# Convolution of the later blocks in 64-token pieces on eight array tiles

## The chip, the cores and the metric

The kernel runs on one core of a Trainium2 chip. The metric is the device time in microseconds (us) of one execution, taken as the median of several runs. A core has a matrix engine (TensorE, PE in the profile, its weight loads PEld), a vector engine (VectorE, DVE), an activation engine (ScalarE, ACT), a general engine (GpSimd, POOL) and a queue that issues transfers (SyncE, SP). Each works through its own list of instructions; semaphores tie the lists together.

## The reference

Two operations follow each other. First a dynamic convolution: each token and head has 7 weights, normalised by a softmax, which are applied to the token and its 6 predecessors, separately for each of 8 heads of 24 channels. Then a feed-forward network with squared relu.

```python
# x: (8, 4096, 192), weight_gen: (8, 4096, 8, 7)
w = softmax(weight_gen, axis=-1)
x_pad = concatenate([zeros((B, 6, D)), x], axis=1)
x_unf = x_pad[:, idx, :].reshape(B, S, K, H, group)     # idx: token + 0..6
y = einsum('bshk,bskhg->bshg', w, x_unf)                # (8, 4096, 192)
h = maximum(y.reshape(32768, 192) @ w_in, 0.0)          # w_in: 192 x 2048
out = (h * h) @ w_out                                   # w_out: 2048 x 192
```

## The kernel before

The 32,768 tokens are cut into 64 sub-blocks of 512 tokens. The first two blocks hold one sub-block each, all others two; there are 33 blocks. A hand-written plan (a string for each block, with "u" for a unit of the first product, "M" for half a quarter of the second, "C" for the convolution of the next block, "B" for bands, "E" and "S" for pieces of the softmax, "L" for a load) sets the order in which every engine's instructions are issued. Blocks from the fifth on use one fixed pattern, and from the one ahead of the ninth block on it is this one:

```python
steady_spread = "MuMuuu" * 2 + "MuCMuuu" + "MuMuuu"
```

So a block is 16 units and eight halves, and the next block's convolution stands between a unit and an L621 half, about the middle of it. The second product that "M" issues belongs to a block issued earlier.

*Softmax and rows.* The softmax weights of a batch are computed with tokens on partitions and stored to memory (`vd`) with 8 slots a head; `wr_load` brings them back for a sub-block as NT = 5 overlapping tiles of 128 tokens, 104 apart (STEP), through SyncE. `x_load` brings the same rows of x as fp16 through GpSimd. Both use `block_load`, which needs one transfer, or two where the first or last tile starts elsewhere. Both are issued two blocks ahead of their block: rows at a block's start, x behind a convolution, since x has two buffers.

*Bands.* `st_band` (L395, VectorE) multiplies the rows with a banded mask, so that the 7 weights of a token become a column of a 128 x 104 band matrix, for each head and tile. `st_bands` does this in one operation for tiles of like offset, up to 4,160 elements a partition.

*Convolution.* `st_conv_spread` (from block 8, FIRST_SPREAD, on; blocks count from 0) multiplies x by the bands on TensorE: 128 token rows contracted, 32 channels out, 104 or 96 tokens wide. Four such matmuls, for two sub-blocks and two heads, go to the four column tiles of the array. The results go to two accumulators `yp` from a ring of three (`ps_h`, shared with the first product), and ScalarE and VectorE copy one each to `y` (L503). A head has 24 channels and a tile 32 places; the spare 8 places of six heads hold a third each of the last two heads. These are computed as a fourth slot and moved to the spare places by transfers on SyncE (L507), and the weights of the first product, `w_p`, are loaded in the same arrangement (`load_w_spread`).

*First product.* `st_unit` issues six matmuls of 64 rows x 512 columns (L572): three slots, each on the upper and the lower half of the array. ScalarE applies the relu (L586), VectorE squares (L590).

*Second product.* `st_mm2` (L621) contracts 128 hidden values in two halves of 64 rows, side by side, 192 columns each; 32 matmuls for an "M". `o_sum` adds the halves, `o_store` writes the result.

*Head.* TensorE starts with 21 matmuls of 512 columns on zeros (`spin`), while the first weights are loaded and the first softmax is computed. GpSimd builds the row selection and the mask, issues loads, and clears `v_big`.

The softmax here doesn't subtract the row's maximum and nothing guards it: scores larger than these inputs give would overflow.

## Time and profile before

| What | us |
|---|---|
| Median of 3 runs | 732.07 |
| Lowest, highest | 731.87, 732.11 |
| Profiled execution, whole | 731.82 |
| Profiled execution, span | 730.0 |

The span runs from the first to the last instruction. Groups of instructions are named by line, engine, operation and tile, with the count behind an x; then come the sum of their times in us, the mean of one in ns, and the idle time of the engine just ahead of them with its releaser. The costliest groups besides those that the next section shows:

```profile
L586 ACT ACTIVATE t<-h 128x1024 f16<-128x1024 f32 x512 | 496.4, 1026 | 60.3 <-PE h L572 58.8
L621 PE MATMUL o<-w_o,g 64*128 64x192 f16 x7872 | 365.5, 243 | 0.1
L590 DVE TENSOR_TENSOR g<-t 128x2048 f16<-128x2048 f16 x225 | 267.4, 1220 | 29.8 <-ACT t L586 29.7
L572 PE MATMUL h<-y,w_p 64*128 64x512 f16 x2400 | 291.7, 376 | 0.0
L395 DVE TENSOR_TENSOR bd<-wr,mask 128x4160 f16<-128x4160 f16 x41 | 94.9, 2316 | 0.1
L395 DVE TENSOR_TENSOR bd<-wr,mask 128x3328 f16<-128x3328 f16 x21 | 39.6, 1884 | 0.1
L493 PE MATMUL yp<-bd,xt 128*32 128x104 f16 x1600 | 27.3, 211 | 0.0
L493 PE MATMUL yp<-bd,xt 128*32 128x96 f16 x400 | 22.7, 206 | 0.0
```

"64*128" is the part of the array that an instruction uses, rows by columns. Busy time is a union: matmuls that overlap count once. The mean of one is its latency, so it says nothing of how close together they can start.

### The profile page before, as it was taken

What the parts mean: (1) busy time and instruction counts of PE and PEld (TensorE: products, weight loads), DVE (VectorE), ACT (ScalarE), POOL (GpSimd) and SP (SyncE); (2) the same over time, 40 slices, a digit from 0 to 9 for tenths busy, and PEclk for the clock granted to TensorE, in tenths of its full rate; (3) what the DMA queues carried; (4) which work ended last, traced back from release to release, by engine and by line L of the source; (5) the groups of instructions that cost most, each with busy time, mean ns of one, the idle gap of its engine ahead of it and who ended that gap; (6) DMA issues with size and microseconds to landing.
All of it is one profiled execution on the core that took longest, in us unless ns stands there. A gap on an engine that the chain in (4) does not pass through costs nothing.

```text
span 730.0 us, 30988 instructions
## 1 busy us (share of the span) xinstructions
PE 724.1 (99%) x14053; PEld 528.0 (72%) x14053; DVE 626.8 (86%) x836; ACT 612.2 (84%) x733; POOL 99.8 (14%) x145
## 2 busy tenths in 40 slices
PE   8999999999999999999999999999999999999998
PEld 4657788777777777777777777777777777777777
DVE  7998998998898988888988888988889988778753
ACT  5999888888888888888888888888888888888883
POOL 8131223321001100011001010010000110001000
PEclk9999999999999999999999999999999999999999
DMA  9555455685345452455432554343544325444012
GB/s 202 118 105 115 82 96 105 132 149 129 86 66 138 90 92 59 82 117 124 76 64 61 136 104 88 56 77 116 107 84 86 57 52 119 66 87 78 30 45 68
DMA packets 125984, 68.30 MB, mean 94 GB/s; under 512 B 85321, under 2 KB 122140, under 8 KB 125340
## 3 DMA queue, kind: packets, MB, share of 16 engines
q0 software_dynamic: 46192, 19.43, 22.9%
q1 hardware_dynamic: 79516, 46.79, 22.4%
q8 instruction: 110, 1.80, 1.1%
q14 instruction: 22, 0.18, 0.1%
q10 hardware_dynamic: 144, 0.10, 0.0%
HBM read 50.18 MB, written 28.70 MB: 108 GB/s over the span
## 4 chain that ended last, share of the span: by engine, by line
PE 98%; ACT 1%; DVE 0%; DMA 0%; issue 0%
PE o L621 47%; PE h L572 44%; PE yp L493 4%; PE h L557 2%; PE yp L527 1%; DMA wg<-in_weight_gen_dram 0%; PE yp L455 0%; ACT y L538 0%; DVE v_first L260 0%; PE pr L372 0%; ACT t L586 0%; DVE ssum L245 0%; ACT ex L238 0%; DVE rcp L252 0%; ACT wr L381 0%
## 5 line engine op out<-in xcount | busy, mean ns | idle before, releaser
L586 ACT ACTIVATE t<-h 128x1024 f16<-128x1024 f32 x512 | 496.4, 1026 | 60.3 <-PE h L572 58.8
L621 PEld LDWEIGHTS <-g 64*128 64x128 f16 (+1 forms) x8032 | 344.3, 94 | 55.0 <-issue 2.2
L621 PE MATMUL o<-w_o,g 64*128 64x192 f16 (+1 forms) x8032 | 380.1, 243 | 0.1
L590 DVE TENSOR_TENSOR g<-t 128x2048 f16<-128x2048 f16 (+1 forms) x287 | 307.4, 1105 | 30.1 <-ACT t L586 29.9
L572 PE MATMUL h<-y,w_p 64*128 64x512 f16 x2400 | 291.7, 376 | 0.0
L572 PEld LDWEIGHTS <-w_p 64*128 64x128 f16 x2400 | 113.9, 94 | 94.7
L395 DVE TENSOR_TENSOR bd<-wr,mask 128x4160 f16<-128x4160 f16 (+4 forms) x90 | 149.6, 1686 | 1.3 <-ACT wr L381 0.7
L637 DVE TENSOR_TENSOR o_sb<-o,o_sb 128x384 f32<-128x384 f32 x123 | 68.4, 556 | 61.1 <-ACT o_sb L635 60.1
L321 POOL DMA_DIRECT2D xt<-in_x_dram x63 | 52.6, 839 | 415.3 <-PE yp L493 362.5
L635 ACT COPY o_sb<-o 128x384 f32<-128x384 f32 x129 | 61.6, 477 | 45.9 <-PE o L621 45.1
L572 PE MATMUL h<-y,w_i 64*128 64x512 f16 x576 | 70.6, 376 | 0.3 <-ACT t L586 0.3
L572 PEld LDWEIGHTS <-w_i 64*128 64x128 f16 x576 | 30.3, 94 | 22.2 <-issue 1.6
L493 PEld LDWEIGHTS <-xt 128*32 128x32 f16 x2000 | 24.6, 95 | 10.6 <-issue 10.6
L260 DVE TENSOR_TENSOR v_big<-ex,rcp 128x112 f16<-128x112 f32 (+5 forms) x180 | 29.9, 237 | 1.7 <-DMA vd<-v_big 0.7
L503 DVE CAST y<-yp 128x1024 f16<-128x1024 f32 x25 | 30.4, 1218 | 0.0
L493 PE MATMUL yp<-bd,xt 128*32 128x104 f16 (+1 forms) x2000 | 28.4, 210 | 0.0
L238 ACT ACTIVATE ex<-wg 128x560 f32<-128x560 f32 (+4 forms) x38 | 25.9, 682 | 1.9 <-DMA wg<-in_weight_gen_dram 1.9
L245 DVE TENSOR_REDUCE ssum<-ex 128x80 f32<-128x560 f32 (+4 forms) x38 | 25.3, 666 | 1.3 <-ACT ex L238 1.3
L503 ACT CAST y<-yp 128x1024 f16<-128x1024 f32 x25 | 25.2, 1007 | 0.0
L252 DVE RECIPROCAL rcp<-ssum 128x80 f32<-128x80 f32 (+4 forms) x38 | 22.8, 600 | 1.3
L311 POOL DMA_DIRECT2D xt<-in_x_dram x7 | 3.9, 554 | 120.9 <-PE yp L493 109.4
L355 POOL DMA_DIRECT2D wr<-v_first x24 | 12.9, 560 | 25.1 <-DVE v_first L260 13.6
(41 smaller groups left out, 115.1 us busy)
## 6 DMA issues: line engine op xcount, KB each, us to landing
out_dram<-o_sb SPq DMA_DIRECT2D x63, 384.0 KB
xt<-in_x_dram POOLq DMA_DIRECT2D x42, 240.0 KB, 4.7
wg<-in_weight_gen_dram SPq DMA_DIRECT2D x4, 1064.0 KB
xt<-in_x_dram POOLq DMA_DIRECT2D x21, 192.0 KB, 5.2
wr<-vd SPq DMA_DIRECT2D x38, 80.0 KB
vd<-v_big SPq DMA_DIRECT2D x5, 512.0 KB
y<-y SPq DMA_DIRECT2D x100, 24.0 KB
wg<-in_weight_gen_dram SPq DMA_DIRECT2D x3, 616.0 KB
```

Source lines behind the costliest of these rows:

```text
L238: nc.scalar.activation(out=self.ex[:, lo:hi].rearrange("p r g k e -> p (r g) k e"), in_=self.wg[:, lo:hi].rearrange("p r (g e) k -> p (r g ...
L260: eng.tensor_tensor(out=bass.AP(tensor=v.tensor, offset=v.offset + lo * H * SL + lo % SL * 2 + g * SL * 2, ap=[list(v.ap[0]), [H * SL + 2, ...
L321: eng.dma_start(out=dst[:, first:last], in_=ap)
L395: nc.vector.tensor_tensor(out=bd_t[j][:, H * lo : H * (lo + len(tiles) * n)].rearrange("p (g m c) -> p g m c", g=shape[1], c=2 * SL), in0= ...
L493: nc.tensor.matmul(out=yp[p0 : p0 + 32, k - k0, a:b], lhsT=x_t[s][:, i, c0 : c0 + 32], rhs=bd[:, head // 2, e, 0 : b - a], start=True, sto ...
L503: copy(out=y[:, k0 : k0 + 2], in_=yp)
L572: nc.tensor.matmul(out=h[:, half], lhsT=w_in_chunk(w, u, slot, half), rhs=y_t[j][r0 : r0 + RT, k], start=(slot == 0), stop=(slot == NK - 1 ...
L586: nc.scalar.activation(out=t1[:, e], in_=h, func=ActF.Relu)
L590: nc.vector.tensor_tensor(out=g[:, a : e + 1], in0=t1[:, a : e + 1], in1=t1[:, a : e + 1], op=AluOp.mult)
L621: nc.tensor.matmul(out=oo[:, cc * Dm : (cc + 1) * Dm], lhsT=g[r0 : r0 + n, cc * P : (cc + 1) * P], rhs=w_o[r0 : r0 + n, fc, :], start=(fc ...
L635: nc.scalar.copy(out=o_sb, in_=o[0][:, c])
L637: nc.vector.tensor_tensor(out=o_sb, in0=o[1][:, c], in1=o_sb, op=AluOp.add)
```

## The change

From block 8 on (sub-blocks from FIRST_HALF = 14), a sub-block's two halves of 256 tokens are laid on the two halves of the partitions. Each half is cut into five tiles of 64 tokens, 56 apart (HSTEP), so a tile holds 8 tokens of overlap. A matmul contracts 64 rows and is 56 tokens wide (32 for the first tile). Eight go to eight tiles of the array: two row halves by four column tiles. The row halves write different banks. Loads and bands follow the new layout, with a mask of its own; one band operation per sub-block. The first rows of a batch's first tile are cleared on VectorE. In the odd heads the 8 spare places now stand ahead of the 24 channels, so that spare places of neighbouring tiles lie together and the fourth slot moves in two transfers instead of four; `w_p` is loaded to match. The warm-up is 68 matmuls of 158 columns.

```diff
+    SP8 = 32 - G
+    HT = TB // 2
+    HSTEP = RT - SL
+    HBASE = HT - RT - (NT - 1) * HSTEP
+    FIRST_HALF = BLOCKS[FIRST_SPREAD][0]
+    mask_h = const.tile([P, HSTEP, 2], f16, name="mask_h")
...
+    def band_mask_half():
+        nc.gpsimd.memset(mask_h, 1.0)
+        for r0 in (0, RT):
+            for sign, base in ((1, SL), (-1, KK - 1 - SL)):
+                nc.gpsimd.affine_select(
+                    out=mask_h[r0 : r0 + RT], in_=mask_h[r0 : r0 + RT],
+                    pattern=[[sign, HSTEP], [0, 2]], compare_op=AluOp.is_ge,
+                    fill=0.0, base=base, channel_multiplier=-sign,
+                )
...
+                own = SP8 * e
                 for a, n, src in (
-                    (0, G, rows(2 * k + e)), (G, RT // 2 - G, rows(SPREAD + e, k))
+                    (own, G, rows(2 * k + e)), ((own + G) % 32, SP8, rows(H - 1 - e, k))
                 ):
...
+    def half_load(j, dst, src, width, eng, before):
+        for n, r0 in enumerate((0, RT)):
+            t0 = (j % NBB) * TB + HT * n + HBASE
+            first = int(t0 < 0 and not before)
+            if first:
+                nc.vector.memset(dst[0:-t0, 0], 0.0)
+                eng.dma_start(out=dst[-t0:RT, 0], in_=src[0 : RT + t0])
+            eng.dma_start(
+                out=dst[r0 : r0 + RT, first:],
+                in_=bass.AP(
+                    tensor=src.tensor, offset=src.offset + (t0 + first * HSTEP) * width,
+                    ap=[[width, RT], [HSTEP * width, NT - first], [1, width]],
+                ),
+            )
...
+        if j >= FIRST_HALF:
+            return half_load(j, x_t[j], x[j // NBB], D, nc.gpsimd, True)
...
+        if j >= FIRST_HALF:
+            return half_load(j, wr, vd_t[j // NBB], H * SL, nc.sync, False)
...
+    def st_band_half(j):
+        bd_t[j] = p_bd.tile([P, H * NT * STEP], f16, name="bd")
+        shape = (P, HP * NT, HSTEP // SL, 2 * SL)
+        nc.vector.tensor_tensor(
+            out=bd_t[j][:, 0 : H * NT * HSTEP].rearrange(
+                "p (g m c) -> p g m c", g=shape[1], c=2 * SL
+            ),
+            in0=wr_t[j].rearrange("p t g c -> p (t g) c").unsqueeze(2).broadcast_to(shape),
+            in1=mask_h.rearrange("p (m c) e -> p m (c e)", c=SL).unsqueeze(1).broadcast_to(shape),
+            op=AluOp.mult,
+        )
...
                 for i in range(NT):
-                    a, b = bounds[i], bounds[i + 1]
+                    t0 = HBASE + HSTEP * i
+                    a, b = max(t0 + SL, 0), t0 + RT
                     for half in (0, 1):
                         s = s0 + half
...
                         for e in (0, 1):
-                            head = 2 * k + e
+                            head = 2 * k + (e if k < NK else 1 - e)
                             p0 = RT * half + 32 * e
-                            c0 = min(G * head, D - 32)
-                            nc.tensor.matmul(
-                                out=yp[p0 : p0 + 32, k - k0, a:b],
-                                lhsT=x_t[s][:, i, c0 : c0 + 32],
-                                rhs=bd[:, head // 2, e, 0 : b - a],
...
-                                tile_position=(0, p0),
-                            )
+                            c0 = G * head - (SP8 if head % 2 else 0)
+                            for n, r0 in enumerate((0, RT)):
+                                nc.tensor.matmul(
+                                    out=yp[p0 : p0 + 32, n, (k - k0) * HT :][:, a:b],
+                                    lhsT=x_t[s][r0 : r0 + RT, i, c0 : c0 + 32],
+                                    rhs=bd[r0 : r0 + RT, i, head // 2, head % 2, HSTEP - (b - a) :],
...
+                                    tile_position=(r0, p0),
+                                )
-            copy(out=y[:, k0 : k0 + 2], in_=yp)
-        for p0 in range(0, P, 32):
-            head = SPREAD + p0 // 32 % 2
-            r0 = p0 + G * head - min(G * head, D - 32)
-            nc.sync.dma_start(out=y[p0 + G : p0 + 32, 0:NK], in_=y[r0 : r0 + G, NK])
+            copy(
+                out=y[:, k0 : k0 + 2].rearrange("p k (n c) -> p n k c", c=HT),
+                in_=yp.rearrange("p n (k c) -> p n k c", c=HT),
+            )
+        for r0 in (0, RT):
+            nc.sync.dma_start(
+                out=y[r0 + G : r0 + RT - G, 0:NK], in_=y[r0 + SP8 : r0 + RT - SP8, NK]
+            )
...
     def st_bands(j):
+        if j >= FIRST_HALF:
+            return st_band_half(j)
...
+        WARM = 158
...
-                nc.tensor.matmul(out=wp, lhsT=warm[:, 0:P], rhs=warm, start=True, stop=True)
+                nc.tensor.matmul(
+                    out=wp[:, 0:WARM], lhsT=warm[:, 0:P], rhs=warm[:, 0:WARM],
+                    start=True, stop=True,
+                )
...
-        spin(21)
+        spin(68)
...
         nc.gpsimd.memset(v_big, 0.0)
+        band_mask_half()
```

## The prediction

> **What bounds the kernel now.** I read the page's busy times first, then the chain of waits, then the waits of TensorE alone, then the convolution itself in the timeline, then the costliest groups.

> ```profile
> PE 724.1 (99%) x14053; PEld 528.0 (72%) x14053; DVE 626.8 (86%) x836; ACT 612.2 (84%) x733; POOL 99.8 (14%) x145
> PE 98%; ACT 1%; DVE 0%; DMA 0%; issue 0%
> PE o L621 47%; PE h L572 44%; PE yp L493 4%; PE h L557 2%; PE yp L527 1%; DMA wg<-in_weight_gen_dram 0%; PE yp L455 0%; ACT y L538 0%; DVE v_first L260 0%; PE pr L372 0%; ACT t L586 0%; DVE ssum L245 0%; ACT ex L238 0%; DVE rcp L252 0%; ACT wr L381 0%
> ```

> TensorE (PE) is busy 99% and is 98% of the chain; the two feed-forward products (L572, L621) are 91% of it. The spread convolution (L493), which the change touches, is 4%: some 29 us at most can be had.

> ```profile
> 155.00:709.00 554.00, 554.00 (x10838) 1.00 0.43 87
> ...
> PE h L572 <- ACT t L586: 0.3, 1, 0.3
> ```

> The first line is TensorE over the stretch that holds all 25 spread convolutions: no idle time, full clock. The second is one of its only four waits in the whole run, all in the head. So a nanosecond off TensorE in this stretch is a nanosecond off the end, unless something else becomes late. One convolution, with what stands around it on all engines:

> ```profile
> 420.04 0.38 PE L572 MATMUL h<-y,w_p 64*128 64x512 f16 x2
> ...
> 420.35 0.96 PEld L493 LDWEIGHTS <-xt 128*32 128x32 f16 x80 [0.42 <-issue]
> 420.35 1.11 PE L493 MATMUL yp<-bd,xt 128*32 128x104 f16 x80
> 420.46 1.02 ACT L586 ACTIVATE t<-h 128x1024 f16<-128x1024 f32 x1 [0.41 <-PE h L572]
> 421.38 1.01 ACT L503 CAST y<-yp 128x1024 f16<-128x1024 f32 x1
> 421.40 1.49 PE L621 MATMUL o<-w_o,g 64*128 64x192 f16 x32
> 422.07 1.22 DVE L503 CAST y<-yp 128x1024 f16<-128x1024 f32 x1
> 422.73 2.11 PE L572 MATMUL h<-y,w_p 64*128 64x512 f16 x18
> ```

> The recorded ends of matmuls are modelled, so I count starts. The last product before starts at 420.04, the convolution at 420.35, the next product at 421.40. Single records in the trace sharpen this (medians of the 25): 306 ns from the last L572 start to the first L493 start, 929 ns from first to last L493 start, 137 ns to the first L621 start; 1,372 ns in all. Inside, four matmuls start 3 to 4 ns apart, and such a group repeats every 47 ns (43 to 44 for the 96-column groups). 104 columns at 512 columns per 213 ns (L572's own spacing) are 43.3 ns, so a group is stream plus 3.5 ns. The first group takes 59, 13 more: its weights were not there yet.

> [...] 306 ns where L572 followed by L621, without a change of tiles, takes 212, so 94 ns going in, and 137 less 43 of streaming, 94, coming out. [...]

> **The change part by part.**

> *Convolution.* Per block, 80 matmuls of 128 rows (104 or 96 columns) become 160 of 64 rows (56 or 32 columns): 4 head pairs, 5 pieces, 8 tiles. So 20 groups of eight replace 20 groups of four. Three floors for a group:
> - stream: 56 columns are 23.3 ns, plus 3.5 gives 26.8; 32 columns 13.3 plus 3.5;
> - issue: where weights wait in the queue, loads start 3.3 ns apart, and load-matmul pairs at the head of a convolution also 3.3 to 3.5, so eight pairs need 27 ns;
> - weights: the 13 ns of the first group fit inside the 27 of the group before.

> Stream and issue meet at 27. As two equal limits disturb each other (the spread inside today's groups grows from 10 to 26 ns over the block), I take 30. First to last start: 13 + 19 x 30 + 27 = 610 ns. Going in stays 306 (another tile shape is still changed to); going out is 94 plus 23 = 117. Sum 1,033 against 1,372: 339 ns less, times 25 is 8.5 us. Bounds: 27 per group gives 396 ns, 9.9 us; no gain at 47; the slow side is in the rivals.

> *What is late next.* After the convolution come one L621 half (1.29 us) and three L572 units. The third needs the accumulator that VectorE's cast frees. Measured from the convolution's start, that cast ends at 2.90 to 2.94 and the unit starts at 3.67 to 3.72, so 0.75 us of room in every block; 0.34 is used. The second unit needs ScalarE's cast, done at 2.04, and starts at 3.02 or later: 1.0 of room. Both hold even if the casts don't move.

> *Bands.* L395 today costs 2,316 ns at 4,160 elements and 1,884 at 3,328, 0.52 ns an element. One operation of 2,240 elements is then 1.32 us, two per block 2.64 against 2.31 + 2.35 = 4.66. VectorE gets 2 us freer in each 22.1 us and casts sooner; no wait of TensorE ends on it, so the gain is 0. The 32-partition clear of a batch's first tile is less than one of these.

> *Transfers.* x and weight rows carry the same 640 rows for 512 tokens, in two transfers of 64 x 5 rows rather than one of 128 x 5 (or two). GpSimd issues four x transfers a block, at 0.55 to 0.86 us each at most 3.4 us, and has idled some 20 us before; they land in about 5 us and are used a block (22 us) later. SyncE issues four row transfers, which no longer split by tile, likewise a block ahead. 0. The fourth slot: four transfers at 0.67 us become two of the same total bytes; today they are issued from 2.1 us after the convolution's last start, when VectorE's cast is done, within 2.83 us. Their reader is the next block's first unit, behind seven units of 0.65 us and four L621 halves of 1.29, some 9.7 us after the convolution. That leaves 4.8 us for the landing, and the two shorten it at most: 0.

> *Casts.* Same 1,024 elements a partition, two runs of 256 exchanged: 0, at most nothing seen.

> *Warm-up.* 21 x 512 = 10,752 columns become 68 x 158 = 10,744. The last warm-up matmul starts before 7 us, and TensorE then waits until 7.73 for VectorE's v_first (0.39 idle). Each matmul adds some 2 ns at full clock: 0.1 us, covered. 0. It also adds 94 instructions ahead of everything else. With the longer convolution a block is 512 load-matmul pairs, 1,024 instructions, four fetch blocks exactly; so each convolution now falls at the same place of a fetch block.

> *GpSimd's second mask*, a clear and four selections of 64 x 112, stands before the x load of sub-block 3. The 128 x 256 selections took 1.24 us each, so 0.5 to 1.24 each, 2.2 to 5.2 in all. GpSimd waits 3.5 us there today (for v_first, until 22.52). Below 3.5: 0. At 5.2 the row transfers behind it are some 1.5 us late, the bands that wait for them too, and the first L527 convolution of block 2 (31.2, bands done at 30.7) loses up to 1 us. I take 0.

> Sum: 8.5 us off 731.82, the profiled execution (span 730.0 and 1.8 around it), which stands 0.25 below the median of the runs: 732.07 - 8.5 = **723.6**.

> **The rivals.**

> *Slower: instructions can't be delivered.* Now a convolution takes 160 instructions in 929 ns, 5.8 ns each; the forecast needs 320 in 0.6 us, 1.9 each. The trace shows 1.6 ns only in bursts of 8, 4.0 over 16, 4.5 over 24, 5.4 over 64 and more; but all these convolutions are held by their streams, so it is a bound from one side. [...] 107 ns are quick, and 256 come at the delivery rate r. It decides from 107 + 256 r = 949, r = 3.3 ns. (949 is today's 929 and the 20 ns saved going out.) At 4.5 the first-to-last time is 1,259 ns, 310 above that: 25 x 0.31 = 7.8 us more, **739.8**. A gap at a fetch-block border, of which each convolution holds at least one, works the same way. For it: nothing in the trace has run this fast. Against it: the 25 convolutions of before crossed such borders at eight different places, and all took 910 to 959 ns.

> *No change: row halves don't overlap fully.* If weight loads on the 64-row tiles hinder one another, groups take 45 to 48 ns, nothing is won: **732**. Against: L621 and L572 run two row halves 3 to 4 ns apart today, at the stream's own pace (79 to 80 ns for 192 columns).

> *Half the gain.* Groups at 38 ns, or one border gap of about 150 ns each: 25 x 0.17, **727.8**.

> *It works but something hidden surfaces* (mask in the head, 1 us): 724.6, within the range of the first.

> **How the numbers follow.** Forecast with its variants 0.58 (721.8 to 726), half gain 0.16, no change 0.06, slower 0.20. The measurement can't tell less than about 0.2% (1.5 us) from nothing. Faster 0.73, same 0.07, slower 0.20. Range 721.5 to 736: it takes in the best bound (722.2), half the gain, no change, and the mild part of the slow case (r up to 3.9).

> **What would show it.** Right: from the last L572 to the first L621 around a convolution about 1.03 us, TensorE still idle nowhere from 155 us on, block period 22.1 falling to 21.7, VectorE's cast ending well before the third unit. Wrong: starts inside a convolution that go slow after the first 64 instructions, or one long gap at the same row each time; a wait of L572 on a cast; or a stall before 31 us.

## The result and the profile after

The changed kernel takes 753.94 us (median of 6 runs, 751.91 to 757.63) where the kernel before takes 732.09 (6 runs, 731.87 to 732.51). The ratio is 1.030, 95% interval 1.028 to 1.033: 22 us slower, where 8.5 us faster were forecast. The range put on record was 721.5 to 736. The profiled execution took 751.91 us with a span of 750.0, so 20.0 more than the span of before. One of the four executions of experiment e1 below took 766.31 us where the others took 746.70 to 748.49; it is left out of e1's ratio, and as the only trace kept of e1 is of that one, e1 is judged by its times alone.

First the page of the changed kernel: busy time with its share of the span, the chain that ended last by engine, and the queue that the page calls "instruction" (packets, MB, share of 16 engines).

```profile
PE 736.4 (98%) x16100; PEld 540.1 (72%) x16100; DVE 583.0 (78%) x828; ACT 612.4 (82%) x733; POOL 120.9 (16%) x186
PE 97%; issue 1%; ACT 1%; DVE 0%; DMA 0%
q8 instruction: 126, 2.06, 1.2%
```

TensorE is still the bound, and it has become busier by 12 us: its busy time was to fall. "issue" has come into the chain. It is time in which the engine waited for nothing that the profile names. The waits of TensorE alone show where (total in us, times, longest):

```profile
PE yp L546 <- issue: 7.5, 18, 0.9
```

L546 is the new convolution. Its groups, and those of the two things beside it that I had priced:

```profile
L546 PE MATMUL yp<-bd,xt 64*32 64x56 f16 (+1 forms) x4000 | 40.3, 190 | 7.7 <-issue 7.5
L453 DVE TENSOR_TENSOR bd<-wr,mask_h 128x2240 f16<-128x2240 f16 x50 | 65.8, 1316 | 2.8 <-DMA wr<-vd 2.5
L556 DVE CAST y<-yp 128x1024 f16<-128x1024 f32 x25 | 30.6, 1225 | 26.6 <-PE yp L546 26.6
```

The bands cost 1.316 us each, as worked out (1.32). VectorE, freed by them, now waits 26.6 us for the convolution at the casts: it is early, TensorE is late. Here is one convolution in the timeline, TensorE only. Each line has the start in us, the length in us and, at its end, the count; a line that merges several shapes names one of them:

```profile
451.98 0.38 PE L628 MATMUL h<-y,w_p 64*128 64x512 f16 x2
452.29 0.96 PE L546 MATMUL yp<-bd,xt 64*32 64x32 f16 x100
454.13 0.64 PE L546 MATMUL yp<-bd,xt 64*32 64x56 f16 x60 [0.88 <-issue]
454.71 0.26 PE L677 MATMUL o<-w_o,g 64*128 64x192 f16 x2
```

A hundred matmuls, then nothing for about a microsecond, then the other sixty. The gap stands after the hundredth matmul in 24 of the 25 convolutions, and its length varies from 0.1 to 1.1 us. The single records show a second loss. These are the start-to-start times of successive groups, in ns, from this kernel and from before:

```
before, four matmuls a group, medians of the 25 convolutions:
59 47 47 47 44 48 48 47 46 44 48 47 46 47 43 47 47 47 47
after, eight matmuls a group, the one convolution that starts at 452.29:
38 27 29 118 67 67 66 67 67 66 67 67 1115 39 31 31 141 67 67
```

The forecast's 27 ns is there, but for four groups only, that is for 64 instructions (each matmul has its own weight load). Then comes a pause of 80 ns, and from there on every group takes 67 ns: 16 instructions at 4.17 ns, loads and matmuls in strict alternation. After the long gap, 64 instructions come quickly once more, and so they do after every gap of 0.2 us or more.

From the last L628 start ahead of a convolution to the first L677 start behind it, the mean is 2,156 ns, against 1,375 before. 25 times the difference is 19.5 of the 20.0 us of span. So nearly the whole loss lies in the convolutions.

### The profile page after: what moved, and what is told of

Its sections match the earlier page's. It is cut to its first block, busy times and chain, and to the rows that moved or that the text cites. A ratio compares the mean times of both kernels' runs of the same rounds, so it can differ in the third digit from the quotient of the medians.

```text
span 750.0 us, 35095 instructions
## 1 busy us (share of the span) xinstructions
PE 736.4 (98%) x16100; PEld 540.1 (72%) x16100; DVE 583.0 (78%) x828; ACT 612.4 (82%) x733; POOL 120.9 (16%) x186
## 4 chain that ended last, share of the span: by engine, by line
PE 97%; issue 1%; ACT 1%; DVE 0%; DMA 0%
PE o L677 46%; PE h L628 43%; PE yp L546 5%; PE h L613 2%; PE yp L583 1%; DMA wg<-in_weight_gen_dram 0%; PE yp L507 0%; ACT y L594 0%; DVE v_first L279 0%; PE pr L411 0%; ACT t L642 0%; DVE ssum L264 0%; ACT ex L257 0%; DVE rcp L271 0%; ACT wr L420 0%
## 5 line engine op out<-in xcount | busy, mean ns | idle before, releaser
L677 PEld LDWEIGHTS <-g 64*128 64x128 f16 (+1 forms) x8032 | 343.6, 94 | 54.4 <-issue 2.3
L677 PE MATMUL o<-w_o,g 64*128 64x192 f16 (+1 forms) x8032 | 379.8, 243 | 0.0
L646 DVE TENSOR_TENSOR g<-t 128x2048 f16<-128x2048 f16 (+1 forms) x287 | 311.2, 1106 | 34.6 <-ACT t L642 29.7
L628 PE MATMUL h<-y,w_p 64*128 64x512 f16 x2400 | 291.7, 376 | 0.0
L628 PEld LDWEIGHTS <-w_p 64*128 64x128 f16 x2400 | 113.8, 94 | 94.8
L350 POOL DMA_DIRECT2D xt<-in_x_dram x100 | 66.5, 684 | 484.6 <-PE yp L546 473.5
L628 PE MATMUL h<-y,w_i 64*128 64x512 f16 x576 | 70.2, 376 | 0.4 <-ACT t L642 0.3
L453 DVE TENSOR_TENSOR bd<-wr,mask_h 128x2240 f16<-128x2240 f16 x50 | 65.8, 1316 | 2.8 <-DMA wr<-vd 2.5
L556 DVE CAST y<-yp 128x1024 f16<-128x1024 f32 x25 | 30.6, 1225 | 26.6 <-PE yp L546 26.6
L546 PEld LDWEIGHTS <-xt 64*32 64x32 f16 x4000 | 34.6, 89 | 21.3 <-issue 20.2
L546 PE MATMUL yp<-bd,xt 64*32 64x56 f16 (+1 forms) x4000 | 40.3, 190 | 7.7 <-issue 7.5
L628 PEld LDWEIGHTS <-w_i 64*128 64x128 f16 x576 | 28.8, 94 | 23.5 <-issue 1.4
L434 DVE TENSOR_TENSOR bd<-wr,mask 128x3328 f16<-128x3328 f16 (+5 forms) x26 | 33.1, 1312 | 1.2 <-ACT wr L420 0.9
L340 POOL DMA_DIRECT2D xt<-in_x_dram x13 | 10.9, 842 | 42.0 <-PE yp L583 42.0
```

Source lines behind the costliest of these rows:

```text
L350: eng.dma_start(out=dst[r0 : r0 + RT, first:], in_=bass.AP(tensor=src.tensor, offset=src.offset + (t0 + first * HSTEP) * width, ap=[[width ...
L434: nc.vector.tensor_tensor(out=bd_t[j][:, H * lo : H * (lo + len(tiles) * n)].rearrange("p (g m c) -> p g m c", g=shape[1], c=2 * SL), in0= ...
L453: nc.vector.tensor_tensor(out=bd_t[j][:, 0 : H * NT * HSTEP].rearrange("p (g m c) -> p g m c", g=shape[1], c=2 * SL), in0=wr_t[j].rearrang ...
L546: nc.tensor.matmul(out=yp[p0 : p0 + 32, n, (k - k0) * HT :][:, a:b], lhsT=x_t[s][r0 : r0 + RT, i, c0 : c0 + 32], rhs=bd[r0 : r0 + RT, i, h ...
L556: copy(out=y[:, k0 : k0 + 2].rearrange("p k (n c) -> p n k c", c=HT), in_=yp.rearrange("p n (k c) -> p n k c", c=HT),)
L628: nc.tensor.matmul(out=h[:, half], lhsT=w_in_chunk(w, u, slot, half), rhs=y_t[j][r0 : r0 + RT, k], start=(slot == 0), stop=(slot == NK - 1 ...
```

## The experiments

The theory that this suggests, D, has two parts. First, TensorE gets no more than one instruction in 4.17 ns, but for 64 that come quickly at the head of a convolution and after a gap. Second, the long gap is a wait for the next packet of instructions. Of these packets the page of before shows:

```profile
q8 instruction: 110, 1.80, 1.1%
```

All packets of this queue have 16,384 bytes, in both kernels. TensorE has 28,106 loads and matmuls before and 32,200 after, so 255.5 for each of the 110 packets and 255.6 for each of the 126: 16 packets more for 4,094 instructions more. From these counts I take a packet to hold 256 of TensorE's instructions. Below, such a packet is a fetch, its 256 instructions are a fetch block, and a border is the place between two blocks, counted from the start of the program. For the gap above, the queue shows a single packet in the stretch from 450.9 to 452.7, and none from there to 454.2:

```profile
q8 instruction: 1, 0.02, 5.8%
```

By the single records this fetch ran from 450.98 to 452.66, and the gap ended at 454.13. In the 24 convolutions the gap ends 1.3 to 1.6 us after a fetch has ended. Counting every load and matmul from the start of the program, the first instruction that waits is number 188 of its 256 in each of the 24. TensorE's list has up to nine instructions of other kinds besides, so those that wait are about the last 64 ahead of the border between two fetch blocks. The fetch begins, in 22 of the 24 to within 0.4 us, when the instruction 64 ahead of the border before that one starts (450.64 for the gap above).

Since each block of the changed kernel holds 1,024 instructions, which are four fetch blocks, the border falls at the same place in every convolution, and the count of warm-up matmuls moves it. That makes a clean test: there are some more or fewer matmuls on zeros in the first microseconds, and nothing else changes. "Row" below is an instruction's place within a convolution of 320.

**e1: 50 instructions more ahead of everything.**

```diff
-        WARM = 158
+        WARM = 116
-        spin(68)
+        spin(93)
```

> The changed kernel with 93 warm-up matmuls of 116 columns rather than 68 of 158: 50 instructions more ahead of everything, nothing else. Each convolution then starts 50 rows later within its 256-row fetch block; the border falls 42 rows ahead of its start and 214 rows into it. Theory D (instructions arrive at 4.17 ns each [...], and the last 64 rows ahead of a border are held until the next fetch block is usable, some 3.0 us after its fetch starts): the long gap of 0.1 to 1.1 us inside each convolution goes, first to last start falls from 1.7 us (mean) to about 1.24, 739 to 741 us. Rival T (eight tiles get in each other's way, and the long gap is a wait of the convolution for data): nothing changes, 752 to 757 us.

Measured: 746.70, 747.84 and 748.49 us, ratio to before 1.0217 (1.0200 to 1.0234). That is some 6 us better than the change, but not the 739 to 741 of theory D. The part of rival T that takes the gap for a wait for data is out, as the warm-up count alone moved the time. Whether eight tiles get in each other's way is left to e4, e6 and e7; why the gain fell short shows in e4.

**e2: 50 instructions fewer.**

```diff
-        WARM = 158
+        WARM = 250
-        spin(68)
+        spin(43)
```

> The changed kernel with 43 warm-up matmuls of 250 columns: 50 instructions fewer ahead of everything. The border falls 58 rows into each convolution and 314 rows in; nearly the whole convolution lies in one fetch block. Theory D: the gap moves from row 200 to about row 250 and grows from 0.5 to about 1.5 us in each convolution, 775 to 781 us. Rival T: nothing changes, 752 to 757 us.

Measured: 765.91 us, ratio 1.0468 (1.0449 to 1.0487). First TensorE's waits, then one convolution in the timeline:

```profile
PE yp L546 <- issue: 23.1, 25, 1.1
```

```profile
202.11 1.19 PE L546 MATMUL yp<-bd,xt 64*32 64x32 f16 x125
204.28 0.42 PE L546 MATMUL yp<-bd,xt 64*32 64x32 f16 x35 [0.98 <-issue]
```

The gap moved from the 100th to the 125th matmul, so by exactly the 50 instructions by which the border moved. It is in all 25 convolutions and has a median of 1.16 us. A wait for data would have stayed at its matmul. The time was 9 us below the lower end of the expected 775 to 781; the gap of 1.16 rather than 1.5 makes up 25 times 0.34, 8.5 us, of that.

**e3: the rest of the change alone**, on the kernel before: fourth slot in two transfers, `w_p` to match, warm-up.

```diff
...
-                            head = 2 * k + e
+                            head = 2 * k + (e if k < NK else 1 - e)
...
-                            c0 = min(G * head, D - 32)
+                            c0 = G * head - (SP8 if head % 2 else 0)
...
-        for p0 in range(0, P, 32):
...
+        for r0 in (0, RT):
+            nc.sync.dma_start(
+                out=y[r0 + G : r0 + RT - G, 0:NK], in_=y[r0 + SP8 : r0 + RT - SP8, NK]
+            )
...
+                    out=wp[:, 0:158], lhsT=warm[:, 0:P], rhs=warm[:, 0:158],
...
+        spin(68)
```

> The kernel before with the rest of the change: fourth slot in two transfers with the places in w_p to match, warm-up of 68 matmuls of 158 columns; convolution, loads and bands as before. Theory D: 731.5 to 732.7 us, no change. Rival L (the transfers or the warm-up cost part of the 22 us): clearly above 733.

Measured: 731.94 us, ratio 1.0004 (0.9995 to 1.0012). To within some 0.1%, 0.9 us, these parts cost and bring nothing, as the prediction had them.

**e4: matmuls half as wide**, on e1. Half of the tokens are left out of the convolution, and the other half is copied in their place.

```diff
-                                    out=yp[p0 : p0 + 32, n, (k - k0) * HT :][:, a:b],
+                                    out=yp[p0 : p0 + 32, n, (k - k0) * HT :][:, a // 2 : b // 2],
...
-                                    rhs=bd[r0 : r0 + RT, i, head // 2, head % 2, HSTEP - (b - a) :],
+                                    rhs=bd[r0 : r0 + RT, i, head // 2, head % 2, HSTEP - (b - a) :][:, 0 : (b - a) // 2],
...
```

> As e1, but each convolution matmul is half as wide (28 or 16 columns; half of the tokens are left out of the convolution, the other half stands in their place; the two copies out of the accumulators become four). The instruction count of TensorE is that of e1. Theory D: steady groups of eight stay at 67 ns and the time stays that of e1, 739 to 741 us. Rival T, if streams on eight tiles hinder each other: groups fall towards 35 to 45 ns and the time to about 730.

Measured: 747.47 us, ratio 1.022 (1.020 to 1.024), the same as e1, but again not the 739 to 741. The steady groups of eight stay at 66 to 67 ns, and three quick ones at 26 to 39; half the columns saved nothing. So the streams aren't the limit. No long gap is left in the convolutions but in the first: 1,711 ns each (median; the mean is 1,725, and 25 times 0.35 is 8.7 us above before). Yet the span (744.2) is 14.2 above. One block shows where most of the rest went:

```profile
337.09 1.47 PE L546 MATMUL yp<-bd,xt 64*32 64x16 f16 x160
338.49 1.49 PE L680 MATMUL o<-w_o,g 64*128 64x192 f16 x32
339.82 2.28 PE L631 MATMUL h<-y,w_p 64*128 64x512 f16 x18
341.77 0.92 PE L680 MATMUL o<-w_o,g 64*128 64x192 f16 x16
```

The 18 matmuls of the first product behind the convolution take 2.28 us, where before they took 2.11. The records put the excess at row 406, behind the 203rd matmul, with 186 ns a block in the mean, 4.6 us in all: that is 256 after row 150, 64 ahead of the next border. A part of the wait had moved out of the convolution into what follows; it fits that the next fetch block now held the other half of the convolution. That is what the expectations for e1 and e4 had left out.

**e5: 40 instructions more than the change**, so that neither fetch block is short.

```diff
-        WARM = 158
+        WARM = 122
-        spin(68)
+        spin(88)
```

> The changed kernel with 88 warm-up matmuls of 122 columns: 40 instructions more ahead of everything than in the change. Rows are then held at rows 160 and 416 after each convolution's start. Theory D: from e4's times between rows, the two fetch blocks concerned last some 3.4 and 3.8 us, [...]so next to no fetch stall is left, and what remains is the arrival of instructions alone: each convolution 1,711 to 1,740 ns against 1,375, 25 times 0.35 = 8.7 us more than before, 740 to 742 us. Rival F (the fetch stall is the whole loss; once it is gone eight tiles pay): 724 to 733 us.

Measured: 742.62 us, just above the expected 740 to 742, ratio 1.0144 (1.0129 to 1.0160). TensorE alone in the timeline, then the convolution's group:

```profile
605.21 0.81 PE L628 MATMUL h<-y,w_p 64*128 64x512 f16 x6
605.95 1.49 PE L546 MATMUL yp<-bd,xt 64*32 64x32 f16 x160
607.38 0.67 PE L677 MATMUL o<-w_o,g 64*128 64x192 f16 x11
```

```profile
L546 PE MATMUL yp<-bd,xt 64*32 64x56 f16 (+1 forms) x4000 | 37.4, 190 | 0.0
```

All 160 go in one run, without idle time. A block repeats every 22.45 us (22.09 before), and a convolution takes 1,734 ns in the mean. 25 times 0.359 is 9.0 us of the 10.9 by which the span (740.9) exceeds before. Another 1.5 lies ahead of the first of the 25, which starts at 156.8 rather than 155.2; 1.0 of it is there at the convolution of block 2 (32.16 rather than 31.20), about half from a warm-up that ended later and half from one wait on "issue" of 0.5 us in the head. The 3.4 and 3.8 us of the expectation lie above the 2.2 to 3.3 us that the changed kernel took from the start of a fetch to the end of a gap. Rival F is out: with no wait left in the convolutions the change still loses.

**e6: half the matmuls**, on the change. One of each pair of slots is left out.

```diff
-            for k in ks:
+            for k in (k0,):
...
```

> The changed kernel with only one of each pair of slots convolved, copied to both (the convolution of the other two slots is left out): 80 matmuls of the same shape on eight tiles rather than 160. Theory D: 64 instructions quick (107 ns), a pause of 80, the other 96 at 4.17 ns, so 0.6 us from first to last start and about 1.0 us in all, 25 times 0.35 less than before, 722 to 725 us; so half the instructions save some 25 times 0.7 where half the columns (e4) saved nothing. If tiles were the limit, half the columns should have saved as much as half the matmuls.

Measured: 724.74 us, as expected, ratio 0.9903 (0.9888 to 0.9918). One convolution:

```profile
526.37 0.81 PE L629 MATMUL h<-y,w_p 64*128 64x512 f16 x6
527.11 0.82 PE L546 MATMUL yp<-bd,xt 64*32 64x32 f16 x80
527.87 0.83 PE L678 MATMUL o<-w_o,g 64*128 64x192 f16 x16
```

A convolution takes 1,063 ns, 671 less than in e5 for 160 instructions less: 4.2 ns each. Half the columns saved nothing, half the matmuls save all this.

**e7: the kernel before, matmuls half as wide.** Half of the tokens are left out of the convolution, and the other half is copied in their place.

```diff
-                                out=yp[p0 : p0 + 32, k - k0, a:b],
+                                out=yp[p0 : p0 + 32, k - k0, a // 2 : b // 2],
...
-                                rhs=bd[:, head // 2, e, 0 : b - a],
+                                rhs=bd[:, head // 2, e, 0 : (b - a) // 2],
...
```

> The kernel before (128 rows, four tiles) with convolution matmuls half as wide, 52 or 48 columns (half of the tokens left out of the convolution, the other half copied in their place; four copies rather than two). Streams alone would give groups of four at 25 ns. Theory D: after the first 64 instructions groups of four come at 8 x 4.17 = 33 ns, 0.7 us from first to last start, 1.13 in all, 725 to 727 us. Rival T (the limit belongs to 64-row tiles): groups at 25 ns throughout, 0.5 us, 720 to 722 us.

Measured: 724.94 us, at the lower edge of what theory D expected, ratio 0.9905 (0.9888 to 0.9921). First one convolution in the timeline, then the group-to-group times of a convolution, in ns:

```profile
525.24 0.81 PE L573 MATMUL h<-y,w_p 64*128 64x512 f16 x6
525.98 0.84 PE L493 MATMUL yp<-bd,xt 128*32 128x52 f16 x80
526.75 0.92 PE L622 MATMUL o<-w_o,g 64*128 64x192 f16 x18
```

```
40 25 25 25 25 25 26 34 34 36 34 32 33 34 33 33 34 56 36
```

The first eight groups, which are 64 instructions, follow each other at 25 ns but for the first step; then come 33, which is 8 times 4.17. So the limit shows on 128-row tiles too, at the same time for an instruction; it doesn't belong to the eight tiles. In the kernel before, the 47 ns of a group of four cover it: 33 are needed. There is no pause of 80 ns here. In the records the 66th instruction starts 227 ns after the first, and 214 in the changed kernel; the first 64 took 0.20 us here and 0.13 there. It fits that the next instruction arrives 0.21 to 0.23 us after the start, whatever the 64 take; that is a reading of these two numbers, and nothing else here shows it.

Two things stay open. Every matmul here comes with a load of 32 columns, so the runs give 8.33 ns for a pair, and not what loads and matmuls in another proportion would take. And that the limit lies in the arrival of instructions rather than in the engine is inferred: 64 go quickly at the head of a convolution and after a gap, with four tiles as with eight, so what is used up counts instructions and not tiles. What sets the count of 64, and what a fetch does between its landing and the end of a gap, no view shows; that the gap is a wait for a fetch rests on the place and the times of the gaps alone.

No version that beats the kernel before came out of this. The best placed form of the change (e5) is 1.4% slower than it.

## Why the prediction was wrong

The step that failed is "issue" in the three floors of a group: "load-matmul pairs at the head of a convolution also 3.3 to 3.5, so eight pairs need 27 ns". That was read off the first four pairs of a convolution of before. As a sustained floor it is 67 ns, for 16 instructions at 4.17. With it, the first-to-last time becomes 1.30 us instead of 0.61, and the sum per convolution 1.73 instead of 1.03 (e5): a loss of 9.0 us in place of a gain of 8.5. e4, e6 and e7 show it. That loss alone, to about 741 us, lies outside the range. A second term was put at nothing in the forecast, the wait at a fetch border; it cost 10.6 us more (e1, e2 and e5 show it).

The other steps:

- The rival "instructions can't be delivered" named a limit of this kind and the point from which it decides (3.3 ns). Its sum is 107 ns for 64 quick instructions, and 256 more at r each; the 64 were not shown by the trace of before, and are by that of the changed kernel (four groups 27 to 38 ns apart, then 118). Its rate of 4.5 gave 739.8; with the wait moved out of the convolutions the kernel takes 742.6 (e5), of which 1.5 is head. So the limit was named rightly, but that the price came so near is in part luck: with the measured 4.17 its sum, 107 + 256 x 4.17, gives 1,175 ns from first to last start, where 1,302 were measured; the pauses (80 ns behind the first 64, and one of 26 later), which it left out, account for most of the rest. The rival was given a chance of 0.20 only, though the trace of before had nothing against such a rate: all its bursts were short or bound by their streams, as the text itself says, and a bound from one side is no argument for the other.
- The fetch border was priced at "about 150 ns each" under "half the gain" (whose sum is slightly off: 0.339 less 0.15 is 0.19, not 0.17), and otherwise folded into the slow rival without a price. It cost 422 ns a convolution on average (2,156 less 1,734), 10.6 us: over half of the loss. "The 25 convolutions of before crossed such borders at eight different places" was true, but in those crossings 256 instructions took 3.5 us or more. In the changed kernel TensorE went on 2.2 to 3.3 us after the start of a fetch (3.15 for the gap shown), and before none had to wait. With 320 instructions in 1.3 us that margin is gone: in e2 TensorE waited 23.1 us in all at such borders.
- "Each convolution now falls at the same place of a fetch block" was right and turned out to be the useful line: it made the warm-up count a probe. Both signs of the slow case that the prediction named came true: starts that go slow after the first 64 instructions, and one long gap at the same row.
- Going in 306 and out 117: measured 306 and 127. The 94 ns that going in takes beyond the 212 of L572 followed by L621 stayed, as said.
- Bands, casts, fourth slot, row transfers and warm-up at 0: right. e3 shows it of the fourth slot and the warm-up; of the others no experiment was made, but no wait of TensorE in the changed kernel ends on them, and VectorE is idle at the casts. GpSimd's mask selections took 0.63 us each but for one of 1.72, 3.8 in all, a little above the 3.5 of room; block 2's convolution starts 0.3 later than before (31.50), of which 0.15 were there already at the first selection of rows.
- That a nanosecond of TensorE in this stretch is a nanosecond of the end: right, with the sign turned (19.5 of 20.0 us).

## What to carry to other kernels

Splitting matmuls to fill more tiles of the array lost here, where TensorE got no more than one instruction in 4.17 ns (after the first 64). Before such a split, compare the count of loads and matmuls times the sustained time of one with the time that the streams need. In this case that is 33 against 47 ns a group before, and 67 against 27 after. A spacing read within a burst of up to 64 instructions said nothing here of the sustained supply; for the supply, look for a stretch of more than 64 instructions that nothing else bounds, or make one. Where a few hundred short instructions stand together, look also at how long each stretch of 256 takes (3.5 us or more with a convolution of before, without a stall), and move the border with some instructions elsewhere before believing a comparison.
